# Attention output stage: reversed-half operand for the denominators, tails on GpSimd, and a feature chain moved behind the low parts

## The chip, the cores and the metric

The kernel runs on one core of one Trainium2 chip. A core has a matrix engine (TensorE; PE in the profile, and PEld for its weight loads), three engines for elementwise work (VectorE or DVE, ScalarE or ACT, GpSimd or POOL), queues that start DMA transfers (SP, and also ACT and POOL), the on-chip memory SBUF and the accumulators PSUM. The metric is the time of one execution on the device in microseconds, as the median of several runs.

## The reference

One transformer block with 2048 tokens of width D = 640, in float32. A conditioning vector gives shifts, scales and gates. The attention is linear, with 32 heads of 20 dimensions:

```python
pq = jnp.einsum("bhsd,hdf->bhsf", q, w_phi)
pk = jnp.einsum("bhsd,hdf->bhsf", k, w_phi)
phi_q = jnp.concatenate([_softmax(pq, axis=-1), _softmax(-pq, axis=-1)], axis=-1)
phi_k = jnp.concatenate([_softmax(pk, axis=-1), _softmax(-pk, axis=-1)], axis=-1)
kv = jnp.einsum("bhsf,bhsd->bhfd", phi_k, v)
z  = jnp.einsum("bhsf->bhf", phi_k)
num = jnp.einsum("bhqf,bhfd->bhqd", phi_q, kv)
den = jnp.einsum("bhqf,bhf->bhq", phi_q, z)[..., None] + 1e-6
o = num / den
```

Its output goes through `wo`, a gate and a residual. A second layer norm and a squared-ReLU layer (640 to 1728 to 640) with its own gate and residual follow.

A head's features are two softmaxes, of `pq` and of `-pq`. With unnormalised exponentials `e0`, `e1`, their sums `r0`, `r1`, and the scalar products `d0`, `d1` of the exponentials with `z`, the denominator is `d0/r0 + d1/r1 + 1e-6`. The kernel multiplies it by `r0*r1`, so that one reciprocal is enough: `dd = d0*r1 + d1*r0 + 1e-6*r0*r1`, and the factors for the two halves are `r1/dd` and `r0/dd`. Both the denominators and the factors pair a half with the *other* half's sum: these are the crossed multiplications.

## The kernel before

Tokens are worked in 16 tiles of 128 (`t`), and in 8 pairs of tiles (`j`). Matrix products are made from float32 numbers split into a high and a low part, with three terms each (`three`: high by high, high by low, low by high). Roughly:

- From 0 to 250 us: folding of the weights, normalisation, and K, V, Q projections of all tiles. The exponentials of Q (`e`) of tiles 0 to 11 (`KEPT = 12`) are stored to DRAM (`esp`) and read back as tiles `el`; those of tiles 12 to 15 stay in SBUF (`eq`), and for 13, 14 and 15 the chain of maximum, minimum and subtraction (`q_chain`), the exponentials (`exps`, ScalarE) and the sums (`q_sums`) are made within the next stage.
- From 250 to 385 us: the attention output stage, which the change touches.
- From there to the end: the squared-ReLU layer in 8 pairs (`up`, `acc` in the profile).

The output stage has, for each tile: `e_prod` (L878: the product with `z` into `scr`, its sums per head `dn` on VectorE, then the denominators on GpSimd, L887 to L891), `e_recip` (L897: reciprocal and the two factors, into `dn`, on VectorE), and `e_scale` (L930), which is `e_tail` (L907: heads 30 and 31, 80 columns, into `ut`) and `e_main` (L919: the other 30 heads, 1200 columns, into `ezb`), both on VectorE. For each pair: `tail_turn` and `tail_num` (L936, L943: transpose and product of the tails on TensorE, copies on ScalarE), `tr_e` (L951: transposes of `ezb` on TensorE, copies `ept` on ScalarE), `num` (numerators, into PSUM `numa`, `numb`, `numc`), `num_hi` (ScalarE writes the high parts of `ot`), `num_lo` (the low parts of `ot`: from pair 2 on a subtraction on VectorE, shown as L90, which reads the PSUM tiles last), and `do_wo` (the product of `ot` with `wo` for half `i` of the pair and column group `h`, 15 matmuls each; other TensorE work is hung into it at given terms).

The loop `for j in range(NB)` writes out an order by hand for TensorE, VectorE, ScalarE and GpSimd: each engine does its instructions in the order of the program. SP's queue is ordered by a planner. With `b = 2j+5` and `c = 2j+6`, round `j` issues `e_prod(b)`, `e_recip(b-1)`, `e_scale(b-1)`, `do_wo(j,0,0)` and `(0,1)`, `e_prod(c)`, `e_recip(b)`, `e_scale(b)`, for `j` in 1 and 3 a `q_chain` of tile 13 or 14, then `do_wo(j,1,0)`, `num(j+1)` and `num_hi(j+1)`, and within `do_wo(j,1,1)` `num_lo(j+1)`. The exponentials that follow that `q_chain` come in round `j+1`, behind `do_wo(j+1,0,0)`. In round 5 `q_chain(15)` comes behind the scaling of tile 14. `load_e` reads `el` tiles from DRAM, some three tiles ahead, into buffers that an earlier tile's `e_scale` has to leave first; `plus_x` adds `x` to the stored attention output by a DMA from GpSimd's queue. PSUM's bank `tp` serves `numc` and, next, the tail's transposes.

Of the kernel before, what the change touches and what calls it, by code (L numbers as in the profile page):

```python
# [8 lines left out]
F32 = mybir.dt.float32  # L9
# [3 lines left out]
ALU = mybir.AluOpType  # L13
AX = mybir.AxisListType

P = 128
S = 2048
D = 640
H = 32
DH = 20  # L20
F = 1728
NT = S // P
# [13 lines left out]
KEPT = NT - POSTPONED  # L36
# [1 line left out]
PLAIN = 2  # L38
DEALT = range(NT // 2)
DIRECT = 2  # L40
POWERS = NT
LAST = 3
W_AT = (
    *range(21),
# [9 lines left out]
def kernel(  # L54
# [19 lines left out]
    nc = tc.nc  # L74
# [3 lines left out]
    def mm(o, terms, first=True, last=True, skip=False):  # L78
        for i, (a, b) in enumerate(terms):
            nc.tensor.matmul(  # L80
                o, a, b,
                start=first and i == 0, stop=last and i == len(terms) - 1,
                skip_group_check=skip,
            )

    def three(ah, al, bh, bl):
        return [(ah, bh), (ah, bl), (al, bh)]
# [10 lines left out]
    const = ctx.enter_context(tc.tile_pool(name="const", bufs=1))  # L98
# [79 lines left out]
    rs_q = pc.tile([P, NT, 2 * H], F32, name="rs_q")  # L178
# [80 lines left out]

    cs = const.tile([P, NC], F32, name="cs")  # L260
    ce = const.tile([P, NC], F32, name="ce")
    fill = const.tile([P, 8], F32, name="fill")
    mone = fill[:, :1]
    nc.gpsimd.memset(mone, -1.0)
    nc.scalar.activation(ce, c_t, AF.Exp, scale=-1.0)
    nc.vector.tensor_scalar(ce, ce, 1.0, None, op0=ALU.add)
    nc.vector.reciprocal(ce, ce)
# [169 lines left out]
    def spread(t, e, nm):  # L437
        mx = small([P, 2, H], "mx", f"mx{nm}")
        nc.vector.tensor_reduce(mx[:, 0], heads(t), axis=AX.X, op=ALU.max)
        nc.vector.tensor_reduce(mx[:, 1], heads(t), axis=AX.X, op=ALU.min)  # L440
        for s in (1, 0):
            nc.vector.tensor_tensor(heads(e[:, s]), heads(t), over(mx[:, s]), op=ALU.subtract)
# [32 lines left out]
    def q_chain(t, whole=True):  # L475
        if t < KEPT:
            EQ[t] = tok2(f"q{t % 2}", f"eq{t}")
        e = EQ[t]
        spread(PQ[t], e, f"q{t}")
        if whole:  # L480
            exps(e)
            q_sums(t)
# [232 lines left out]
    for t in range(2, NT - 2):  # L715
        j, i = divmod(t, 2)
# [12 lines left out]
        p = proj("v", t, *([(1, 0, lambda: t1(j + 1, 4))] if t == NT - 3 else []))  # L729
# [136 lines left out]
    def load_e(t):  # L866
        if t >= KEPT:
            if t < NT:
                ET[t] = EQ[t]
            return  # L870
        ET[t] = tok2(("k", "k", f"x{t // 3 % 2}")[t % 3], f"el{t}")
        nc.sync.dma_start(flat(ET[t]), ESP[t])
# [2 lines left out]
    SCR = [flat(tok2("w", f"scr{i}")) for i in range(2)]  # L875
    DN, DD = {}, {}

    def e_prod(t):  # L878
        if t >= NT:
            return  # L880
        z = SCR[t % 2]
        nc.vector.tensor_tensor(z, flat(ET[t]), flat(zb), op=ALU.mult)  # L882
        dn = DN[t] = small([P, 2, H], "dn", f"dn{t}", 3)
        nc.vector.tensor_reduce(dn.rearrange("p s h -> p (s h)"), heads(z), axis=AX.X, op=ALU.add)  # L884
        rs = rs_q[:, t].rearrange("p (s h) -> p s h", s=2)
        dd = DD[t] = small([P, H], "dd", f"dd{t}")
        nc.gpsimd.tensor_tensor(dd, rs[:, 0], rs[:, 1], op=ALU.mult)  # L887
        nc.gpsimd.tensor_scalar(dd, dd, 1e-6, None, op0=ALU.mult)
        for s in range(2):
            nc.gpsimd.tensor_tensor(dn[:, s], dn[:, s], rs[:, 1 - s], op=ALU.mult)  # L890
            nc.gpsimd.tensor_tensor(dd, dd, dn[:, s], op=ALU.add)  # L891
        if t >= POWERS:
            nc.gpsimd.tensor_tensor(dd, dd, mone.to_broadcast([P, H]), op=ALU.pow)
            for s in range(2):
                nc.gpsimd.tensor_tensor(dn[:, s], rs[:, 1 - s], dd, op=ALU.mult)

    def e_recip(t):  # L897
        if t >= NT or t >= POWERS:
            return
        rs = rs_q[:, t].rearrange("p (s h) -> p s h", s=2)  # L900
        nc.vector.reciprocal(DD[t], DD[t])
        for s in range(2):
            nc.vector.tensor_tensor(DN[t][:, s], rs[:, 1 - s], DD[t], op=ALU.mult)

    UT = {}

    def e_tail(t):  # L907
        if t >= NT:
            return
        if t % 2 == 0:  # L910
            u = row("s3", f"ut{t // 2}")
            UT[t], UT[t + 1] = u[:, :80], u[:, 80:160]
        nc.vector.tensor_tensor(
            UT[t].rearrange("p (s h d) -> p s h d", s=2, d=DH),
            ET[t][:, :, 600:].rearrange("p s (h d) -> p s h d", d=DH),
            DN[t][:, :, 30:, None].to_broadcast([P, 2, 2, DH]), op=ALU.mult
        )
# [12 lines left out]
    def e_scale(t):  # L930
        e_tail(t)
        e_main(t)
# [72 lines left out]
    def wo_part(j, i, h, a, b):  # L1005
        t = 2 * j + i
        if h == 0 and a == 0:
            PWO[t] = pj(f"pwo{t}")
            AT[t] = row("s2", f"at{t}")
        s = slice(i * P, (i + 1) * P)  # L1010
        cs_, n = slice(*CUT[h]), CUT[h][1] - CUT[h][0]
        terms = []
        for g in range(5):
            w, o = WO[g], OT[j]
            terms += three(o[:, g, 0, s], o[:, g, 1, s], w[:, 0, cs_], w[:, 1, cs_])
        mm(PWO[t][h][:, :n], terms[a:b], first=(a == 0), last=(b == 15))
        if b == 15:
            nc.scalar.activation(AT[t][:, cs_], PWO[t][h][:, :n], AF.Copy)
            if h:
                nc.scalar.dma_start(A1[t], AT[t])  # L1020
# [199 lines left out]
    SPREAD, SUMS = {1: 1, 3: 2}, {3: 1, 4: 2}  # L1220
    ln0 = None
    for j in range(NB):
        nxt = j + 1 < NB
        b, c = 2 * j + 5, 2 * j + 6
        turns = {1: ((0, 0, 11), (0, 0, 15), (0, 1, 4), (0, 1, 15)), 6: ((0, 1, 2), (0, 1, 8), (0, 1, 15), (1, 0, 15)),
                 0: ((0, 1, 4), (0, 1, 10), (1, 0, 3), (1, 0, 15))}.get(j, ((0, 0, 6), (0, 0, 11), (0, 0, 15), (0, 1, 15)))
        todo_ = (lambda: tail_turn(j + 1), lambda: tail_num(j + 1), lambda: tr_e(j + 1, range(3)), lambda: tr_e(j + 1, (3, 4)))

        def hooks(i, h):
            return [(at, f) for (i_, h_, at), f in zip(turns, todo_) if nxt and (i, h) == (i_, h_)]  # L1230
        if j == 4:
            load_x1(0)
            load_dealt(0)
        if j < 5:
            p_load()
        if j != 5:
            e_prod(b)
        e_recip(b - 1)
        e_scale(b - 1)
        if j == 6:  # L1240
            mod_sum(5, gate_b)
        if j == 5:
            q_chain(KEPT + 3, False)
        load_e(b + 2)
        do_wo(j, 0, 0, *hooks(0, 0))
        if j - 1 in SPREAD:
            exps(EQ[KEPT + SPREAD[j - 1]])
        if j == 5:
            exps(EQ[KEPT + 3])
            q_sums(KEPT + 3)  # L1250
            e_prod(b)
        do_wo(j, 0, 1, *hooks(0, 1))
        if j == 7:
            t2(0, 0)
            t2(0, 1)
        if j == 4:
            ln0 = ln_dealt(0)
            next(ln0)
            next(ln0)
        if j == 6:  # L1260
            next(ln0)
            turn(0, 0)
            turn(0, 1)
        if 1 <= j < 6 and j != 4:
            p_hi()
        if j == 5:
            next(ln0)
        if j in SUMS:
            q_sums(KEPT + SUMS[j])
        e_prod(c)  # L1270
        if j != 5:
            e_recip(b)
            e_scale(b)
        if j in SPREAD:
            q_chain(KEPT + SPREAD[j], False)
        do_wo(j, 1, 0, *hooks(1, 0))
        if j == 7:
            t2(0, 2)
            t2(0, 3)
        if nxt:  # L1280
            num(j + 1)
            num_hi(j + 1)
        if j == 4:
            next(ln0)
            next(ln0)
            next(ln0)
        if j == 5:
            p_hi()
        do_wo(j, 1, 1, b=8)
        if j == 7:  # L1290
            t2(0, 4)
            p = tp("gbt")[:NC, :P]
            nc.tensor.transpose(p, gate_b, ident)
            nc.scalar.activation(gate_r, p, AF.Copy)
            nc.sync.dma_start(GD[1], gate_r)
            nc.sync.dma_start(gb_b, GD[1].rearrange("c p -> (c p)")[None, :].to_broadcast([P, D]))
        if not nxt:
            do_wo(j, 1, 1, a=8)
        if nxt:
            do_wo(j, 1, 1, a=8, b=11)  # L1300
            num_lo(j + 1)
            do_wo(j, 1, 1, a=11)
        if j == 5:
            e_recip(b)
            e_scale(b)
        load_e(c + 2)
        if j:
            plus_x(j - 1)
        if j == 5:
            p_lo(4)  # L1310
            p_load(4)
        if j == 6:
            p_hi(4)
            p_lo(5)
            p_load(3)
        if j == 7:
            p_load(2)
# [485 lines left out]
```

## Time and profile before

| what | value |
|---|---|
| median of 3 runs | 756.0 us (755.9 to 756.18) |
| the profiled execution | 755.36 us, of it the span 753.7 us |
| clock that TensorE was granted | 1.00 |
| DVE, 268 to 302.7 us | 33.42 of 34.70 us busy |
| POOL, 268 to 302.7 us | 21.68 of 34.70 us busy |
| whole span: ACT, POOL | 61%, 23% |

The span is what the hardware profiler recorded on the core; the execution's time has 1.66 us more around it. TensorE is busy for nearly all of the span, and the chain that ended last runs over TensorE for 89% of it and over VectorE for 8%, the latter between 255 and 334 us. In rows of the timeline the first number is the start in us, the second the time from there to the end, then engine, line of the kernel, operation, output and input, shape, the number of instructions merged into the row and, in brackets, how long the engine was idle before it and what ended that.

### The profile page before, as it was taken

What the parts mean: (1) busy time and instruction counts of PE and PEld (TensorE: products, weight loads), DVE (VectorE), ACT (ScalarE), POOL (GpSimd) and SP (SyncE); (2) the same over time, 40 slices, a digit from 0 to 9 for tenths busy, and PEclk for the clock granted to TensorE, in tenths of its full rate; (3) what the DMA queues carried; (4) which work ended last, traced back from release to release, by engine and by line L of the source; (5) the groups of instructions that cost most, each with busy time, mean ns of one, the idle gap of its engine ahead of it and who ended that gap; (6) DMA issues with size and microseconds to landing.
All of it is one profiled execution on the core that took longest, in us unless ns stands there. A gap on an engine that the chain in (4) does not pass through costs nothing.

```text
span 753.7 us, 15321 instructions
## 1 busy us (share of the span) xinstructions
PE 745.8 (99%) x5854; PEld 728.1 (97%) x5854; DVE 604.3 (80%) x1115; ACT 457.3 (61%) x1065; POOL 169.9 (23%) x362
## 2 busy tenths in 40 slices
PE   9999999999999999899999999999999999999998
PEld 9999999999999998789899999999999999999997
DVE  6598987988999899998755768787777776777766
ACT  5767666677863356447677756585574756647431
POOL 3000101000100337646303030132221313213110
PEclk9999999999999999999999999999999999999999
DMA  9811432343432254652986475997677777667460
GB/s 330 331 36 80 154 96 75 106 140 106 140 106 70 71 183 150 154 137 96 208 216 205 132 219 215 281 320 203 187 207 200 212 190 219 187 181 213 129 185 36
DMA packets 58796, 126.39 MB, mean 168 GB/s; under 512 B 7438, under 2 KB 16403, under 8 KB 58723
## 3 DMA queue, kind: packets, MB, share of 16 engines
q1 hardware_dynamic: 38636, 79.20, 32.0%
q0 software_dynamic: 17504, 40.90, 21.9%
q10 hardware_dynamic: 2583, 5.30, 1.9%
q8 instruction: 46, 0.75, 0.4%
q14 instruction: 27, 0.22, 0.1%
HBM read 100.74 MB, written 29.89 MB: 173 GB/s over the span
## 4 chain that ended last, share of the span: by engine, by line
PE 89%; DVE 8%; POOL 1%; ACT 1%; issue 0%; ACTq 0%; POOLq 0%
PE up L80 25%; PE acc L80 18%; PE pk L80 9%; PE pv L80 9%; PE pq L80 8%; PE pwo L80 5%; PE acc3x L80 5%; PE kvp L459 3%; DVE dn L884 2%; DVE scr L882 2%; DVE ezb L924 2%; PE te L958 1%; PE foldk L284 1%; PE ta L366 1%; PE foldq L284 1%; POOL dn L890 1%
## 5 line engine op out<-in xcount | busy, mean ns | idle before, releaser
L80 PE MATMUL up<-h,w 128*128 128x256 f32 x1640 | 204.6, 276 | 0.1
L80 PEld LDWEIGHTS up<-h,w 128*128 128x128 f32 x1640 | 196.4, 188 | 0.7 <-DVE h L90 0.5
L1352 ACT ACTIVATE ft<-up,b_t 128x256 f32<-128x256 f32 x104 | 48.9, 470 | 96.0 <-PE up L80 95.6
L80 PE MATMUL acc<-w,ra 128*128 128x384 f32 x452 | 97.4, 335 | 0.0
L80 PE MATMUL pwo<-wo,ot 128*128 128x384 f32 (+1 forms) x480 | 78.9, 314 | 3.0 <-DVE ot L90 3.0
L1353 DVE TENSOR_TENSOR ft<-ft 128x256 f32<-128x256 f32 x104 | 44.2, 425 | 42.9 <-ACT ft L1352 41.4
L80 PEld LDWEIGHTS pwo<-wo,ot 128*128 128x128 f32 x480 | 69.5, 188 | 6.5 <-DVE ot L90 3.6
L80 PE MATMUL pq<-wq,hT 128*128 128x384 f32 (+1 forms) x480 | 75.6, 312 | 0.0
L80 PEld LDWEIGHTS acc<-w,ra 128*128 128x128 f32 x452 | 72.7, 188 | 0.9 <-DVE ra L90 0.6
L80 PE MATMUL pk<-wk,hT 128*128 128x384 f32 (+1 forms) x480 | 72.7, 308 | 0.0
L80 PEld LDWEIGHTS pq<-wq,hT 128*128 128x128 f32 x480 | 71.1, 188 | 0.6 <-issue 0.2
L80 PE MATMUL pv<-wv,hT 128*128 128x384 f32 (+1 forms) x480 | 71.6, 307 | 0.0
L80 PEld LDWEIGHTS pk<-wk,hT 128*128 128x128 f32 x480 | 70.5, 188 | 0.4 <-issue 0.2
L80 PEld LDWEIGHTS pv<-wv,hT 128*128 128x128 f32 x480 | 70.0, 188 | 0.0
L90 DVE TENSOR_TENSOR ra<-ft,ra 128x384 fp32r<-128x384 f32 (+2 forms) x86 | 36.8, 448 | 32.7 <-ACT ra L1376 20.0
L1462 POOL DMA_DIRECT2D ring_a<-td_a x34 | 18.5, 543 | 117.4 <-PE acc L80 106.3
L1376 ACT ACTIVATE ra<-ft 128x384 fp32r<-128x384 f32 x48 | 25.2, 526 | 28.4 <-DVE ft L1353 22.4
L80 PE MATMUL acc3x<-w,ra 128*128 128x256 f32 x231 | 39.5, 278 | 0.0
L80 PEld LDWEIGHTS acc3x<-w,ra 128*128 128x128 f32 x231 | 37.1, 188 | 0.0
L1367 DVE TENSOR_TENSOR ft<-ft 128x128 f32<-128x128 f32 x136 | 33.3, 286 | 1.2
L450 DVE TENSOR_REDUCE sk<-ek 128x64 f32<-128x1280 f32 x16 | 23.7, 1484 | 12.8 <-ACT ek L445 10.8
L343 POOL TENSOR_SCALAR sma<-sma 128x2 f32<-128x2 f32 x6 | 1.7, 292 | 137.3 <-ACT xb L342 137.3
(270 smaller groups left out, 1475.7 us busy)
## 6 DMA issues: line engine op xcount, KB each, us to landing
ring_c<-td_c POOLq DMA_DIRECT2D x34, 384.0 KB, 3.8
ring_a<-td_a POOLq DMA_DIRECT2D x34, 384.0 KB, 3.5
ring_b<-td_b POOLq DMA_DIRECT2D x34, 256.0 KB, 3.4
esp<-eq SPq DMA_DIRECT2D x12, 640.0 KB
el<-esp SPq DMA_DIRECT2D x12, 640.0 KB
rw<-in_w SPq DMA_DIRECT2D x23, 320.0 KB
wm<-in_w_mod SPq DMA_DIRECT2D x20, 320.0 KB
xb<-in_x SPq DMA_DIRECT2D x8, 640.0 KB
```

Of the source, the lines that this page charges most:

```text
L80: nc.tensor.matmul(o, a, b, start=first and i == 0, stop=last and i == len(terms) - 1, skip_group_check=skip,)
L90: (eng or nc.vector).tensor_tensor(out_lo, full, hi.bitcast(F32), op=ALU.subtract)
L284: nc.tensor.matmul(p[g // 3][:, (g % 3) * 120 : (g % 3) * 120 + n], r, bd_t[:120, g * 120 : g * 120 + n], start=True, stop=True,)
L450: nc.vector.tensor_reduce(s, heads(flat(e)), axis=AX.X, op=ALU.add)
L459: nc.tensor.matmul(kvp[g // 4][64 * c : 64 * c + 64, a : a + 2 * n].rearrange("p (s n) -> p s n", s=2), v[:, u], e[:, :, o : o + n], start ...
L882: nc.vector.tensor_tensor(z, flat(ET[t]), flat(zb), op=ALU.mult)
L884: nc.vector.tensor_reduce(dn.rearrange("p s h -> p (s h)"), heads(z), axis=AX.X, op=ALU.add)
L1352: nc.scalar.activation(r, p, AF.Relu, bias=b1_t[:, f : f + 1])
L1353: nc.vector.tensor_tensor(r, r, r, op=ALU.mult)
L1367: nc.vector.tensor_tensor(t[:, o], t[:, a], t[:, b], op=op)
L1376: nc.scalar.activation(a[:, 0, :3], t[:, :3], AF.Copy)
L1462: nc.gpsimd.dma_start(RING[j, n, r], TD[n][r].bitcast(F32R))
```

## The change

It does six things:

1. In `e_prod` one GpSimd multiplication of 64 elements replaces two of 32: the second operand is read with its halves exchanged (`crossed`).
2. In `e_recip` one VectorE multiplication of 64 elements replaces two of 32, by the same operand.
3. From tile 6 on (`POOL_TAILS`) `e_tail` runs on GpSimd.
4. In `do_wo(j,0,0)` the ten terms with the high part of `ot` come first and the five with its low part last.
5. The `q_chain` of rounds 1 and 3 is issued behind `num_lo` of the round, and that of round 5 ahead of the reciprocal and scaling of tile 14.
6. A path of `e_prod` with powers that no tile took (`POWERS = NT`) goes, with a constant of -1 that GpSimd wrote for it.

```diff
-POWERS = NT
+POOL_TAILS = 6
...
-    fill = const.tile([P, 8], F32, name="fill")
-    mone = fill[:, :1]
-    nc.gpsimd.memset(mone, -1.0)
+    const.tile([P, 8], F32, name="fill")
...
+    def crossed(t):
+        a = rs_q[:, t]
+        return bass.AP(tensor=a.tensor, offset=a.offset + H, ap=[a.ap[0], [-H, 2], [1, H]])
...
+        nc.gpsimd.tensor_tensor(dn, dn, crossed(t), op=ALU.mult)
         for s in range(2):
-            nc.gpsimd.tensor_tensor(dn[:, s], dn[:, s], rs[:, 1 - s], op=ALU.mult)
             nc.gpsimd.tensor_tensor(dd, dd, dn[:, s], op=ALU.add)
...
         nc.vector.reciprocal(DD[t], DD[t])
-        for s in range(2):
-            nc.vector.tensor_tensor(DN[t][:, s], rs[:, 1 - s], DD[t], op=ALU.mult)
+        nc.vector.tensor_tensor(DN[t], crossed(t), DD[t][:, None, :].to_broadcast([P, 2, H]), op=ALU.mult)
...
-        nc.vector.tensor_tensor(
+        (nc.gpsimd if t >= POOL_TAILS else nc.vector).tensor_tensor(
             UT[t].rearrange("p (s h d) -> p s h d", s=2, d=DH),
...
+        if (i, h) == (0, 0):
+            terms = [x for k, x in enumerate(terms) if k % 3 < 2] + terms[2::3]
...
-        if j != 5:
+        if j == 5:
+            q_chain(KEPT + 3, False)
+        else:
             e_prod(b)
         e_recip(b - 1)
         e_scale(b - 1)
...
-        if j == 5:
-            q_chain(KEPT + 3, False)
...
-        if j in SPREAD:
-            q_chain(KEPT + SPREAD[j], False)
         do_wo(j, 1, 0, *hooks(1, 0))
...
         if j == 5:
             e_recip(b)
             e_scale(b)
+        if j in SPREAD:
+            q_chain(KEPT + SPREAD[j], False)
```

More of the change, by code (lines that the diff above doesn't have):

```diff
@@ L888, in e_prod @@
         nc.gpsimd.tensor_scalar(dd, dd, 1e-6, None, op0=ALU.mult)
+        nc.gpsimd.tensor_tensor(dn, dn, crossed(t), op=ALU.mult)
         for s in range(2):
-            nc.gpsimd.tensor_tensor(dn[:, s], dn[:, s], rs[:, 1 - s], op=ALU.mult)
             nc.gpsimd.tensor_tensor(dd, dd, dn[:, s], op=ALU.add)
-        if t >= POWERS:
-            nc.gpsimd.tensor_tensor(dd, dd, mone.to_broadcast([P, H]), op=ALU.pow)
-            for s in range(2):
-                nc.gpsimd.tensor_tensor(dn[:, s], rs[:, 1 - s], dd, op=ALU.mult)
     def e_recip(t):
-        if t >= NT or t >= POWERS:
+        if t >= NT:
             return
-        rs = rs_q[:, t].rearrange("p (s h) -> p s h", s=2)
         nc.vector.reciprocal(DD[t], DD[t])
-        for s in range(2):
-            nc.vector.tensor_tensor(DN[t][:, s], rs[:, 1 - s], DD[t], op=ALU.mult)
+        nc.vector.tensor_tensor(DN[t], crossed(t), DD[t][:, None, :].to_broadcast([P, 2, H]), op=ALU.mult)
     UT = {}
```

## The prediction

> **What bounds the kernel now.** I read the page first: its busy table says that TensorE (PE) works through the whole span.
>
> ```profile
> span 753.7 us, 15321 instructions
> PE 745.8 (99%) x5854; PEld 728.1 (97%) x5854; DVE 604.3 (80%) x1115; ACT 457.3 (61%) x1065; POOL 169.9 (23%) x362
> ```
>
> So an engine that is made faster is worth what TensorE waits for it, and no more. The diff touches only the attention output stage, so I asked next for busy times in stretches of it (engine, busy us, number of instructions; then clock, DMA share and GB/s), and for the waits between 255 and 390 us (who waited for whom: total, times, longest).
>
> ```profile
> 268.00:302.70 34.70, 34.70 (x260) 30.20 (x258) 33.42 (x46) 20.71 (x47) 21.68 (x42) 1.00 0.48 160
> 347.00:364.00 17.00, 17.00 (x129) 15.67 (x128) 14.85 (x24) 12.16 (x28) 13.29 (x31) 1.00 0.49 112
> ```
> ```profile
> PEld pwo L80 <- DVE ot L90: 3.6, 2, 2.8
> PE pwo L80 <- DVE ot L90: 3.0, 2, 2.5
> ```
>
> The columns are PE, PEld, DVE, ACT, POOL. In this stage VectorE (DVE) is nearly as full as TensorE: 33.42 of 34.70 us. TensorE waits for it twice, 3.0 us in total; its weight loads, which run ahead, count 3.6. The timeline shows the two places, and what DVE did just before the first.
>
> ```profile
> 300.39 2.33 PE L80 MATMUL pwo<-wo,ot 128*128 128x256 f32 x17
> 305.18 0.96 PE L80 MATMUL pwo<-wo,ot 128*128 128x384 f32 x4 [2.46 <-DVE ot L90]
> 334.18 0.96 PE L80 MATMUL pwo<-wo,ot 128*128 128x384 f32 x4 [0.53 <-DVE ot L90]
> ```
> ```profile
> 299.34 0.29 DVE L903 TENSOR_TENSOR dn<-rs_q,dd 128x32 f32<-128x32 f32 x2
> 299.67 0.24 DVE L913 TENSOR_TENSOR ut<-el,dn 128x80 f32<-128x80 f32 x1
> 299.83 1.46 DVE L924 TENSOR_TENSOR ezb<-el,dn 128x1200 f32<-128x1200 f32 x1
> 301.21 0.81 DVE L439 TENSOR_REDUCE mxq<-eq 128x32 f32<-128x640 f32 x1
> 304.45 0.68 DVE L90 TENSOR_TENSOR ot<-numa,ot 128x512 fp32r<-128x512 f32 x1
> 305.97 1.48 DVE L882 TENSOR_TENSOR scr<-el,zb 128x1280 f32<-128x1280 f32 x1
> ```
> ```profile
> 299.21 0.60 ACT L981 ACTIVATE ot<-numa 128x512 fp32r<-128x512 f32 x1 [0.53 <-PE numa L80]
> 300.57 0.38 ACT L981 ACTIVATE ot<-numc 128x256 fp32r<-128x256 f32 x1
> 331.50 0.38 ACT L981 ACTIVATE ot<-numc 128x256 fp32r<-128x256 f32 x1
> ```
>
> ScalarE (ACT) had the high parts of `ot` at 299.81 and 300.95. The low parts (L90, `num_lo(2)`) began only at 304.45, because `q_chain(13)` stands ahead of them in DVE's hand-written order: 304.45 - 301.21 = 3.24 us. TensorE has used its last high terms at 300.39 + 2.33 = 302.72 and stands still until 305.18. The second wait is the same thing one `q_chain` later. **The moved `q_chain` is the heart of this change.** The rest frees DVE time.
>
> **The change part by part.**
>
> *Moving `q_chain` behind `num_lo` (j = 1 and 3).* DVE leaves `ezb` of tile 7 at 299.83 + 1.46 = 301.29, earlier still by what the small edits save (below, 0.9): 300.4. `num_lo(2)` takes 305.97 - 304.45 = 1.52, so it ends at 301.9, before TensorE asks at 302.72. The wait of 2.46 goes. Nothing is late in its place at once: `q_chain(13)` runs from 301.9 to 305.2, and the product of tile 9 starts there, not at 305.97. ACT's exponentials of tile 13 come in the next round:
>
> ```profile
> 310.46 0.75 ACT L445 ACTIVATE eq<-eq 128x640 f32<-128x640 f32 x1
> ```
>
> With TensorE 2.46 earlier that is 308.0, 2.8 us after their input is there. If DVE ran later than that, every copy behind them on ACT would wait.
>
> *The order of terms in `do_wo(j, 0, 0)`.* Ten high terms instead of two come before the first low one: no instruction more. It gives `num_lo` eight more matmuls of slack, 8 x 2.62 / 15 = 1.4 us by the chain's row of a run of 15.
>
> ```profile
> 312.45 2.62 PE pwo L80 x15
> ```
>
> By itself it would take 1.4 of the 2.46. Here it is cover for the rounds that follow.
>
> *One operation for two in `e_recip` (16 tiles, DVE).* Two 32-element multiplications and the step to the next cost 299.67 - 299.34 = 0.33. The trace has no 64-element one with a backwards read. Its neighbours are 0.188 (mean) at 32 elements and, above, 0.24 at 80:
>
> ```profile
> L903 DVE TENSOR_TENSOR dn<-rs_q,dd 128x32 f32<-128x32 f32 x32 | 4.7, 188 | 0.5
> ```
>
> Interpolated: 0.22; with the same gap of 0.04 ahead of the next (299.34 + 0.29 to 299.67), 0.26, so 0.07 a tile is saved. From both sides: as cheap as the 32-element one (0.10 saved) or, if the reversed order were read at half speed, as dear as the two together (nothing saved). I take 0.07.
>
> *The tail on GpSimd (POOL) from tile 6 (10 tiles).* DVE's step of 299.83 - 299.67 = 0.16 goes. With the above it is 0.49 - 0.26 = 0.23 a tile. POOL gets a two-input operation of 80 elements; an undisturbed one of 32 takes 0.25, and beside DVE the same kind takes far more:
>
> ```profile
> 293.91 0.25 POOL L890 TENSOR_TENSOR dn<-dn,rs_q 128x32 f32<-128x32 f32 x1 [1.12 <-DVE dn L884]
> 294.49 0.31 POOL L890 TENSOR_TENSOR dn<-dn,rs_q 128x32 f32<-128x32 f32 x1
> 294.88 1.29 POOL L891 TENSOR_TENSOR dd<-dd,dn 128x32 f32<-128x32 f32 x1
> 296.14 1.50 POOL L887 TENSOR_TENSOR dd<-rs_q 128x32 f32<-128x32 f32 x1
> ```
> ```profile
> 294.61 1.46 DVE L924 TENSOR_TENSOR ezb<-el,dn 128x1200 f32<-128x1200 f32 x1
> 295.99 1.54 DVE L882 TENSOR_TENSOR scr<-el,zb 128x1280 f32<-128x1280 f32 x1
> ```
>
> Each POOL operation that meets DVE's `ezb` or `scr` ends just behind it (294.88 + 1.29 = 296.17 beside an `ezb` to 296.07). So a tail costs POOL between 0.3 and 1.5. It stands behind the sums of the next tile in POOL's queue, and so ends up to 3 us after its `ezb` began, when the next `scr` is over. POOL's queue holds: of 299.83 - 294.61 = 5.2 us a tile it has about 1.1 free before its L890. DVE's subtractions out of PSUM don't hold it:
>
> ```profile
> 360.73 0.69 DVE L90 TENSOR_TENSOR ot<-numa,ot 128x512 fp32r<-128x512 f32 x1 [0.47 <-ACT ot L981]
> 360.88 0.25 POOL L890 TENSOR_TENSOR dn<-dn,rs_q 128x32 f32<-128x32 f32 x1
> ```
>  Who waits: the transposes of the tails on TensorE, a round later, and the loads of `el` into the same buffers. For tile 6 the tail is done by 297.6, behind a `scr`; for tile 7, whose `ezb` is followed by `num_lo(2)`, by 300.4 + 0.4 = 300.8. Their transposes come six matmuls after 302.72, at about 303.7. Costed at nothing, with cover of 2.9 us there and 1 us at the tightest place (tile 13, below).
>
> *One POOL operation less in `e_prod`.* 16 x about 0.3 on an engine that is 23% busy: nothing.
>
> *`q_chain(15)` before tile 14's scaling (j = 5).* Both have a round to spare: TensorE shows no wait from 347 to 364. Nothing, at most 1 us if ACT's copies fall behind.
>
> *The removed memset* is 0.1 us of POOL in the first microseconds: nothing.
>
> **The sum.** TensorE wins 2.46 + 0.53 = 2.99 if DVE keeps up. I followed DVE through the rounds:
>
> ```profile
> 318.56 1.48 DVE L882 TENSOR_TENSOR scr<-el,zb 128x1280 f32<-128x1280 f32 x1
> 330.28 0.81 DVE L439 TENSOR_REDUCE mxq<-eq 128x32 f32<-128x640 f32 x1
> 334.98 1.48 DVE L882 TENSOR_TENSOR scr<-eq,zb 128x1280 f32<-128x1280 f32 x1
> 340.87 1.49 DVE L487 TENSOR_REDUCE rs_q<-eq 128x64 f32<-128x1280 f32 x1 [0.66 <-ACT eq L446]
> 348.64 0.41 DVE L90 TENSOR_TENSOR ot<-numc,ot 128x256 fp32r<-128x256 f32 x1
> ```
> ```profile
> 349.17 0.38 PE L940 MATMUL tail<-ident,ut 128*80 128x128 f32 x2
> ```
>
> Up to 301.29 it saves 6 x 0.07 + 2 x 0.23 = 0.9, and each later round 2 x 0.23 = 0.46. Round 2: 305.2 + (318.56 - 305.97) - 0.46 = 317.3 at most (waits for ACT in it shrink too, perhaps to 316.8). Round 3: another 11.72 - 0.46 brings 328.1 to 328.6. There `num_lo(4)` must wait for ACT, whose last high part comes at 331.88 - 2.46 = 329.4; DVE is through at about 330.1, and with the `q_chain` (334.98 - 330.28 less 1.52 = 3.2) starts the next round at 333.3, not 334.98. Round 4 takes 349.05 - 334.98 = 14.07, less 0.46, less the 0.66 for ACT: `num_lo(5)` ends at 346.25. TensorE, 2.99 earlier, comes to the transpose of tail pair 6 at 349.17 - 2.99 = 346.18, and it needs the PSUM bank that `num_lo(5)` reads last. The two meet: a wait of 0.1 to 0.2 there. I take 2.9 us off. Behind 347 TensorE had no wait, ACT and DVE are not full, and the weights' loads follow DVE's releases; all of it moves forward together.
>
> The profiled execution took 755.36 us (span 753.7 and 1.66 around it), 0.64 below the median 756.0. By its own time: 755.36 - 2.9 = 752.5; against the median **753.1 us**, 0.38% less. A difference under 0.2%, 1.5 us, is about what a measurement of this kernel can't tell from none.
>
> **The rivals.**
>
> *The gain is eaten by the port (same).* What is seen in the rows is POOL waiting for DVE. The other way round, DVE's `scr` took 1.54 beside POOL work and 1.48 without, 0.06 more. If each POOL tail slipped in ahead of a big DVE operation and held it for its own 0.34, DVE would lose 0.34 for tiles 6 to 13 by round 4: 2.7 us. `num_lo(5)` would end at 349.0, TensorE would wait 2.7 at the tail's transpose, and the time would be 755.8; with half of it, 754.4. For it: DVE and TensorE meet there in any case. Against it: the 0.06. [...]
>
> *A load comes late (slower).* The tails of tiles 6 and 7 now also hold the buffers into which `el` of tiles 9 and 10 is loaded. Now these are issued as `ezb` ends:
>
> ```profile
> 296.09 5.54 SPq L872 DMA_DIRECT2D el<-esp  x2
> 308.50:309.50 1.00, 1.00 (x12) 1.00 (x11) 0.97 (x4) 0.92 (x2) 0.36 (x2) 1.00 0.62 126
> 311.14 1.54 DVE L882 TENSOR_TENSOR scr<-el,zb 128x1280 f32<-128x1280 f32 x1
> ```
>
> The second is issued at 296.09 + 5.54 - 0.33, or 301.3; the DMA traffic that it shares with others thins out in the stretch from 308.5 to 309.5 (share 0.62), and tile 10's product reads it at 311.14 (at 310.1 in the changed kernel). I have the tail of tile 7 done at 300.8, so the load keeps its time. Were it held until `scr` of tile 9 had passed, it would be issued at 306.7 and land up to 8.2 later, near 315; DVE would be 4.8 late, TensorE would wait about 4.7 by tail pair 6, and the sum be 3.0 gained and 4.7 lost: 757.7. It decides from an issue about 1 us later than now, and turns the sign from about 4.
>
> *Something behind the stage does not move along (between).* The weights for the next phase are on their way while this one ends, and ACT waits for them once:
>
> ```profile
> 377.42 1.37 ACT L1050 ACTIVATE w<-rawt 128x640 fp32r<-128x640 f32 x2 [0.40 <-DMA rw<-in_w]
> ```
>
> If they landed when they do now, ACT would be held almost 3 us and the start of the next phase with it, all but what its copies can catch up: 755.4 if that is 0.6. Against it: DVE frees their buffers some 3 us earlier too. A part of it, 1 to 2 us, is likelier than all.
>
> **How the numbers follow.** The forecast, 752.4 to 754.2, has 0.69; its low end is 756.0 less the 3.6 of the weight loads' wait. The port has 0.15 (754.4 to 755.8), the transfers 0.10 (754.2 to 755.4), the late load 0.06 (756.5 to 758). Below 754.5: 0.69, half of the port's and half of the transfers', 0.81; above 757.5: some 0.04; the rest 0.15. The range from 752.4 to 755.5 leaves out less than 0.2.
>
> **What would show it.** Right: no wait of `pwo` for DVE `ot` near 302 and 331; `num_lo(2)` directly behind `ezb` of tile 7; `dn` of 64 elements near 0.22; POOL tails of 0.3 to 1.5. Wrong: waits at a `tail` transpose or at a `scr` for DMA, DVE operations stretched by 0.3 beside POOL, or a later ACT `w` wait.

## The result and the profile after

The changed kernel takes 751.55 us (median of 6 runs, 751.01 to 752.85) beside 756.09 us before (6 runs, 755.4 to 756.7); the ratio is 0.9941 with a 95% interval of 0.9928 to 0.9954. That is 4.5 us less, where 2.9 was forecast and 752.4 was the low end of the range. The profiled executions differ by less: 751.83 against 755.36 us.

The page of the changed kernel (span; busy time and number of instructions by engine):

```profile
span 750.1 us, 15320 instructions
PE 744.9 (99%) x5854; PEld 728.3 (97%) x5854; DVE 601.4 (80%) x1089; ACT 457.5 (61%) x1065; POOL 169.0 (23%) x355
```

Of the list of waits between 255 and 390 us, what TensorE and its weight loads still wait for:

```profile
PEld tail L936 <- POOL rn L1160: 0.7, 1, 0.7
PE tail L936 <- POOL rn L1160: 0.4, 1, 0.4
```

Both waits of `pwo` for `ot` are gone. The wait left is at the transpose of tail pair 6. The timeline of DVE at the place of the old 2.46 us wait:

```profile
298.72 1.41 DVE L920 TENSOR_TENSOR ezb<-el,dn 128x1200 f32<-128x1200 f32 x1
300.05 0.68 DVE L90 TENSOR_TENSOR ot<-numa,ot 128x512 fp32r<-128x512 f32 x1
301.25 0.41 DVE L90 TENSOR_TENSOR ot<-numc,ot 128x256 fp32r<-128x256 f32 x1
301.58 0.81 DVE L437 TENSOR_REDUCE mxq<-eq 128x32 f32<-128x640 f32 x1
```

The low parts now come straight behind `ezb` of tile 7, and the chain of tile 13 (L437) behind them. TensorE's timeline at both old waits, after and then before:

```profile
300.12 3.09 PE L80 MATMUL pwo<-wo,ot 128*128 128x256 f32 x21
303.05 0.38 PE L936 MATMUL tail<-ident,ut 128*80 128x128 f32 x2
...
328.31 3.09 PE L80 MATMUL pwo<-wo,ot 128*128 128x256 f32 x21
331.24 0.38 PE L936 MATMUL tail<-ident,ut 128*80 128x128 f32 x2
```
```profile
306.11 0.42 PE L940 MATMUL tail<-ident,ut 128*80 128x128 f32 x2
306.28 1.12 PE L80 MATMUL pwo<-wo,ot 128*128 128x384 f32 x5
...
331.32 2.33 PE L80 MATMUL pwo<-wo,ot 128*128 128x256 f32 x17
...
335.11 0.41 PE L940 MATMUL tail<-ident,ut 128*80 128x128 f32 x2
```

The same 21 matmuls lie between the first row and the transpose. Before, that took 306.11 - 300.39 = 5.72 us, and now 303.05 - 300.12 = 2.93: 2.79 are won where the recorded idle time was 2.46. In round 4 it is 3.79 against 2.93: 0.86 for 0.53. **Each wait cost 0.33 us more than its idle time.** A part of that is a second wait for DVE, which the list of waits before has in a row of its own. Below it, from the timelines before, the weight load of the transpose and DVE's last low part:

```profile
PEld tail L940 <- DVE ot L90: 0.6, 2, 0.3
```
```profile
306.11 0.15 PEld L940 LDWEIGHTS tail<-ident,ut 128*80 128x80 f32 x2 [0.29 <-DVE ot L90]
```
```profile
305.64 0.41 DVE L90 TENSOR_TENSOR ot<-numc,ot 128x256 fp32r<-128x256 f32 x1
```

The transpose needs the bank that the last low part reads, and starts 0.47 us after the start of that operation (306.11 - 305.64), in round 4 as well (335.11 - 334.64). By the single starts in the trace it comes 0.31 us behind the start of the last of the four matmuls, where the changed kernel has 0.17: that is some 0.13 of the 0.33. Most of the rest lies at the first matmul behind the wait, whose successor starts 0.28 and not 0.18 behind it, and in the way idle time is counted, from the end of a matmul beside which the next would have begun: the two ahead of the wait start 0.17 us apart and take 0.33 and 0.34 each.

### The profile page after: what moved, and what is told of

It is laid out like the page before. It is cut to its first block, busy times and chain, and to the rows that moved or that the text cites. A ratio compares the mean times of both kernels' runs of the same rounds, so it can differ in the third digit from the quotient of the medians.

```text
span 750.1 us, 15320 instructions
## 1 busy us (share of the span) xinstructions
PE 744.9 (99%) x5854; PEld 728.3 (97%) x5854; DVE 601.4 (80%) x1089; ACT 457.5 (61%) x1065; POOL 169.0 (23%) x355
## 4 chain that ended last, share of the span: by engine, by line
PE 98%; ACT 1%; DVE 1%; POOL 0%; issue 0%; ACTq 0%; POOLq 0%
PE up L80 25%; PE acc L80 18%; PE pq L80 9%; PE pk L80 9%; PE pv L80 9%; PE pwo L80 9%; PE acc3x L80 5%; PE kvp L457 3%; PE te L954 2%; PE numa L80 1%; PE foldk L282 1%; PE numb L80 1%; PE ta L364 1%; PE foldq L282 1%; PE warm L625 1%; PE mrow L586 1%
```

## The experiments

Theory A, formed from these rows: the waits were priced too low, at 3.0 and not at 2.79 + 0.86 = 3.65, and the rest is spread between runs. Theory B: the saved operations are worth about 1.5 us that no wait shows.

### The changed kernel again

No edit.

> The changed kernel once more, beside the kernel before on the same chip. Theory A (the waits were priced too low: each of the two cost TensorE its recorded idle time and about 0.3 us more, until weight loads and matmuls overlap again, so 3.6 us and not 3.0 are won, and 0.6 is lost at the transpose of tail pair 6; the rest of the 4.5 us is spread between runs): 3.5 to 4.0 us under the kernel before, and the two profiles differ by the same. Theory B (another part of the change is worth about 1.5 us that the profile's waits don't show): 4.3 us or more under it, here too.

Measured: 751.69 us beside 755.95, 4.3 less (ratio 0.9938, 0.9926 to 0.9951). That is more than the 3.5 to 4.0 of theory A, and what theory B expected (4.3 or more). Something was missing in A.

### The chains moved back

```diff
+        if j in SPREAD:
+            q_chain(KEPT + SPREAD[j], False)
         do_wo(j, 1, 0, *hooks(1, 0))
...
             e_scale(b)
-        if j in SPREAD:
-            q_chain(KEPT + SPREAD[j], False)
```

> The changed kernel with the feature chains of tiles 13 and 14 back ahead of the low parts; all else stays. Theory A: in round 2 TensorE waits about 2 us again, and not at the first low term, which the new order of terms has moved back, but at the transpose of tail pair 3, which stands six terms into the product and needs the PSUM bank that the low parts release; later DVE is no longer the last to come. 1.7 to 2.6 us slower than the changed kernel, 1.2 to 2.0 under the kernel before. Theory B (the operations saved on DVE make the gain): under 1 us slower than the changed kernel. The prediction's own sum would give 3.0 less the slack of eight terms and 0.9 of DVE's time: about 0.7 us slower.

Measured: 755.2 us, 3.5 slower than the changed kernel, where theory A had 1.7 to 2.6; against before 0.9986 (0.9977 to 0.9994). Theory B is out: with every saved operation in place, the gain is nearly gone. The place of the wait is as expected, its price is not. TensorE's timeline:

```profile
304.50 0.39 PE L936 MATMUL tail<-ident,ut 128*80 128x128 f32 x2 [1.89 <-DVE ot L90]
304.65 1.76 PE L80 MATMUL pwo<-wo,ot 128*128 128x384 f32 x5
306.21 0.91 PE L942 MATMUL tail<-kvd,ept 80*128 80x40 f32 x4
306.91 1.57 PE L80 MATMUL pwo<-wo,ot 128*128 128x384 f32 x4
```

The wait stands at the transpose, six terms into the product. But the matmuls behind it are slow: 1.76 us for five that took 1.12 before. Busy times by stretch say why (the number behind POOL's is the granted clock):

```profile
304.50:305.00 0.50, 0.49 (x4) 0.50 (x5) 0.50 (x1) 0.07 (x1) 0.00 (x0) 0.89 0.97 147
305.00:306.00 1.00, 1.00 (x5) 1.00 (x4) 0.90 (x2) 0.31 (x1) 0.00 (x0) 0.50 0.88 137
307.00:308.00 1.00, 1.00 (x4) 1.00 (x4) 0.93 (x4) 0.30 (x2) 0.49 (x2) 0.50 0.97 255
308.00:309.00 1.00, 1.00 (x9) 0.92 (x9) 1.00 (x1) 0.47 (x2) 0.92 (x2) 0.85 0.19 42
```

**TensorE's clock falls to 0.50** from about 304.9 to 308.3, 3.4 us; it begins 0.4 us after work has begun again. The profile of the kernel before shows 1.00 throughout its span. So theory A became A': idle time, plus 0.33 us, plus a fall of the clock in some executions.

### The move alone, and with the order of terms

The first takes the kernel before and moves the two chains; the second takes the changed kernel, with two operations in `e_recip` and `POOL_TAILS = NT`, so that DVE saves nothing.

> The kernel before with only the two feature chains moved behind the low parts; no operation is saved and no tail is on GpSimd. Theory A: the wait of 2.46 in round 2 goes with its 0.3, but DVE has lost the time for it: it comes about 2 us late to the low parts of pair 5, and TensorE waits for these at the transpose of tail pair 6. 1.0 to 2.0 us under the kernel before. If the move alone were the gain: 3.0 us or more under it. Theory B: under 1 us.

Measured: 753.5 us, 2.45 under before (ratio 0.9965, 0.9953 to 0.9977).

> The changed kernel with the factors by two operations again and all tails on DVE: the moved chains and the order of terms stay, DVE saves nothing. Theory A: as with the move alone, within 0.4 us, because the order of terms gives no slack where a transpose six terms in waits for the bank: 1.0 to 2.0 us under the kernel before. If the order of terms were worth its eight matmuls: 2.4 to 3.0 us under it. Theory B: 1 us or less.

Measured: 752.92 us, 3.0 under before (0.996, 0.9947 to 0.9972). Both gain more than expected. A' accounts for it: from the first transposes of `ezb` (`te`) to the first `up`, the first profile before takes 117.8 us and these two take 116.0 and 115.7, so 1.8 and 2.1 less; with the 0.7 for the clock that is worked out below it makes 2.5 and 2.8. Their order among themselves isn't clear. Their lists of waits, the move alone first, show that DVE is late again further on:

```profile
PE pwo L80 <- DVE ot L90: 1.3, 2, 1.1
```
```profile
PE tail L938 <- DVE ot L90: 1.7, 2, 1.2
```

The move removes the long wait. Without the saved operations a part of it comes back in rounds 3 and 5, as 1.3 and 1.7 us. The saved operations pay by keeping DVE ahead of that.

### The kernel before once more

> The kernel before once more, for its profile. Theory A': besides idle time and overlap, the wait of about 2.5 us in round 2 lets TensorE's clock fall to 0.50 for some 3.4 us in part of the executions (the profile with the chains moved back showed 0.50 from about 304.9 to 308.2 and matmuls 1.6 us longer there; the profile of before did not). Then a profile of the kernel before that shows 0.50 behind the wait has a span about 1.6 us longer than one that doesn't, and the median lies between the two. Theory B': the clock never falls in the kernel before, and the spread of 755.0 to 757.5 is the start of the kernel (transfers) alone.

Measured: 756.65 us beside 756.28 (ratio 1.0007, 0.9997 to 1.0017). Its profile, by stretch and in TensorE's timeline:

```profile
306.00:307.00 1.00, 1.00 (x5) 1.00 (x4) 0.96 (x2) 0.38 (x1) 0.00 (x0) 0.50 0.98 267
307.00:308.00 1.00, 1.00 (x6) 1.00 (x5) 1.00 (x1) 0.00 (x0) 0.00 (x0) 0.50 1.10 256
```
```profile
304.46 0.97 PE L80 MATMUL pwo<-wo,ot 128*128 128x384 f32 x4 [2.42 <-DVE ot L90]
305.39 0.65 PE L940 MATMUL tail<-ident,ut 128*80 128x128 f32 x2
305.69 1.95 PE L80 MATMUL pwo<-wo,ot 128*128 128x384 f32 x5
```

Same program, same wait, and this time the clock falls behind it: the five matmuls take 1.95 us and not 1.12. From TensorE's first `pk` to the end this execution is 1.23 us longer than the first profile. Its span is only 0.5 longer, since the start of the kernel, with its loads, was 0.73 us shorter in it.

The clock's records in the traces show where the two executions differ. In the three profiles with a fall behind a wait (this one, the chains moved back, and the made wait below) it lasts 3413 ns, and it begins 300.373, 300.373 and 372.053 us after the clock was first full: 88, 88 and 109 times 3413.3 ns. In the first profile before and in that of the changed kernel the clock stays full for 747.519 and 744.106 us, up to a fall behind the last matmul: 219 and 218 times. So each of these five falls began a whole number of stretches of that length (windows, from here on) after the first full clock, and the stretches lay differently against the program in the two executions of the kernel before. What sets the clock no run shows. The window that holds the pause and the next one, in this profile:

```profile
301.97:305.38 3.41, 0.99 (x5) 0.65 (x4) 3.34 (x7) 0.14 (x1) 1.89 (x3) 1.00 0.93 232
305.39:308.79 3.40, 3.40 (x14) 3.38 (x14) 3.33 (x5) 0.68 (x3) 0.38 (x2) 0.50 1.00 222
```

In the first profile a boundary falls into the pause, at 303.87; that follows from its own fall behind the end of the program, at 754.42, which is 132 windows later:

```profile
300.45:303.86 3.41, 2.27 (x19) 1.96 (x17) 3.34 (x5) 0.88 (x3) 3.32 (x5) 1.00 0.42 126
303.87:307.28 3.41, 2.10 (x12) 1.81 (x13) 3.41 (x5) 0.38 (x1) 0.81 (x1) 1.00 1.02 223
754.43:755.40 0.97, 0.00 (x0) 0.00 (x0) 0.00 (x0) 0.00 (x0) 0.00 (x0) 0.50 0.00 0
```

Here TensorE works 0.99 us of the window, and the next one gets half the clock. There the boundary cuts the pause in two, TensorE works 2.27 and 2.10 us, and the clock stays up. In the three profiles with a fall behind a wait the window ahead of it holds 1.89 us of idle time (the chains moved back), 2.42 (this one) and 2.2 (the made wait). In the first profile before the most that a window holds while TensorE still has work is 1.32, in that of the changed kernel 0.9, and no 0.50 follows. The other nine profiles, whose longest recorded waits are 1.2 us, have a mean clock of 0.999 or more.

Each timed execution has its mean clock beside it. 0.5 for 3.4 of 754 us makes 0.998, and so the executions fall into two groups:

| kernel | longest recorded TensorE wait in the stage, us | executions | clock 0.998 or less | median of those | median at 0.999 or more |
|---|---|---|---|---|---|
| before (beside the experiments, three chips) | 2.46 | 55 | 33 | 756.6 | 755.42 |
| chains moved back | 1.89 | 11 | 7 | 755.22 | 754.04 |
| made wait (below) | 2.67 | 10 | 9 | 756.98 | 754.82 (one) |
| move and terms | 1.2 | 6 | 0 | | 752.92 |
| move alone | 1.1 | 5 | 0 | | 753.5 |
| before, wait filled (below) | 0.5 | 11 | 0 | | 754.84 |
| changed (the result and two runs) | 0.5 | 16 | 0 | | 751.7 |

The run above, of the kernel before once more, is not in the table; of its eight executions seven have 0.998 or less. In the kernel before three executions of five have the lower clock, and their median is 1.2 us longer. The first profile had caught one that doesn't.

### The wait filled

The kernel before, with matmuls whose results are not needed, ahead of the third term of round 2:

```diff
+    def keep_warm(j):
+        for _ in range(22):
+            nc.tensor.matmul(PWO[2 * j][1][:, :P], neg, neg, start=True, stop=True)
...
-        do_wo(j, 0, 0, *hooks(0, 0))
+        do_wo(j, 0, 0, *([(2, lambda: keep_warm(j))] if j == 2 else []), *hooks(0, 0))
```

> The kernel before with 22 matmuls of 128 columns that compute nothing needed, put into the wait of 2.46 us in round 2 (into a PSUM bank that is written anew afterwards). More work, and the low parts come no sooner. Theory A': TensorE doesn't rest, so no execution loses clock and the weight loads stay overlapped: 0.3 us under the kernel before if its clock seldom falls, 1.0 to 1.5 under it if it falls in half of the executions or more; no 0.50 in the profile. Theory B' (only the arrival of the low parts counts): equal to the kernel before within 0.3 us, or slower by what the filling overshoots.

Measured: 754.84 us beside 756.28, 1.4 less (ratio 0.9983, 0.9974 to 0.9992), no execution with a reduced clock.

```profile
302.76 2.57 PE L1224 MATMUL pwo<-neg 128*128 128x128 f32 x22
305.61 0.97 PE L80 MATMUL pwo<-wo,ot 128*128 128x384 f32 x4 [0.28 <-DVE ot L90]
```

The low parts come no sooner, and 22 matmuls more make the kernel faster. What they buy is the clock: its share of the gap, 0.6 x 1.2 = 0.7 us. Some 0.6 to 0.7 more stay open. They are not the 0.33, for the four matmuls behind the filling still take 0.97, and the stage is no shorter than in the first profile before, which has the full clock too (118.0 and 117.8 us from the first `te` to the first `up`). The single executions lie between 754.3 and 756.5.

### A made wait

The changed kernel, with six reductions of no use on DVE ahead of the low parts of pair 7:

```diff
+            if j == 6:
+                for k in range(6):
+                    nc.vector.tensor_reduce(small([P, 64], "dly", f"dly{k}", 1), rs_q.rearrange("p t (a b) -> p (t a) b", b=16), axis=AX.X, op=ALU.add)
             num_lo(j + 1)
```

> The changed kernel with six additional DVE reductions of 1024 elements (about 7.5 us in all, results unused) ahead of the low parts of pair 7, where DVE has about 5 us to spare: a made wait of TensorE at the first low term of round 7, about 3 us long. Theory A': the time grows by the recorded idle time and about 0.3 us, and by about 1.6 us more in executions whose clock falls: 4.5 to 5.0 us over the changed kernel if it falls in most. Theory B': it grows by the idle time alone, about 3 us.

Measured: 756.86 us, and the clock reduced in nine of ten executions. Beside it ran the kernel before (756.28), not the changed one; over the 751.7 of the changed kernel in the table it is 5.2.

```profile
377.74 8.27 PE L80 MATMUL pwo<-wo,ot 128*128 128x384 f32 x43 [2.67 <-DVE ot L90]
```
```profile
380.00:382.50 2.50, 2.50 (x14) 2.50 (x13) 2.29 (x4) 0.08 (x1) 0.22 (x1) 0.53 0.65 74
```

A recorded wait of 2.67 us cost about twice its length here, in another round and behind another cause than in the kernel before. That is 0.2 us above the range of theory A'. From the first `te` to the first `up` the profile has 119.4 us, the changed kernel 114.5: 4.9 more.

### The parts that are left

All of these ran beside the changed kernel on one chip, and the later transpose before that on another one, without the changed kernel. The one GpSimd multiplication less, the earlier `q_chain(15)` and the removed memset were not run alone.

> The changed kernel beside the next three on one chip. Theory A' (idle time, 0.33 us of lost overlap behind each wait, and a clock that falls behind a wait of 1.9 us and more in about two of three executions): the clock is full in all its executions; in the kernel before it is reduced in about two of three, those are some 1.1 us longer, and the changed kernel lies 3.6 to 4.0 us under the others. If the clock had nothing to do with it: the two groups of the kernel before don't differ.

Measured: 752.18 us beside 756.3 (0.9945, 0.9932 to 0.9957); clock full in all five.

```diff
-                 0: ((0, 1, 4), (0, 1, 10), (1, 0, 3), (1, 0, 15))}.get(
+                 0: ((0, 1, 4), (0, 1, 10), (1, 0, 3), (1, 0, 15)), 5: ((0, 0, 11), (0, 0, 15), (0, 1, 4), (0, 1, 15))}.get(
```

> The changed kernel with the transposes of tail pair 6 at the eleventh term of round 5's first product and not at the sixth, as round 1 has it (the later hooks of the round move with it). If TensorE's wait of 0.37 there (0.57 with its overlap) is for the PSUM bank that DVE's last low part releases, or for GpSimd, five matmuls (0.9 us) cover it: 0.3 to 0.6 us under the changed kernel, no wait at the transpose. If the wait comes back at the next hook, no change.

> The changed kernel with the transposes of tail pair 6 five terms later, against the changed kernel on the same chip. Its profile before showed no wait there and a stage about 0.45 us shorter; if that is so, the median is 0.3 to 0.6 us under the changed kernel's; if the spread between executions hides it, within 0.3.

Measured: 751.97 us on the other chip (before there: 756.28), and 752.12 against the changed kernel's 752.18 on the common one. The wait at the transpose is gone, and a smaller one stands at the second group of transposes:

```profile
351.17 1.14 PE L954 MATMUL te<-ident,ezb 128*124 128x128 f32 x8 [0.17 <-ACT ept L955]
```

Whether it gains the 0.3 to 0.6 us can't be told from the spread; it isn't a version that is shown to be better.

> The changed kernel with the old order of terms. Theory A': only in round 5 do the low parts come so late that the third term has to wait, 0.3 us, and then the transpose of the tails has that much less to wait; in round 0 the low part comes 0.1 late. 0.1 to 0.5 us slower than the changed kernel, clock full. If the order gives the eight matmuls of cover that the prediction gave it: 0.5 to 1.4 us slower.

Measured: 751.69 us with the old order of terms, 0.5 under the changed kernel and within its spread (751.6 to 754.4 beside 751.25 to 753.17). Neither the expected 0.1 to 0.5 us nor the prediction's slack can be seen. Its list of waits has one row for DVE's `ot`, `PEld` alone:

```profile
PEld pwo L80 <- DVE ot L90: 0.4, 1, 0.4
```

> The changed kernel with all tails on DVE, and nothing else undone. DVE does 0.16 to 0.2 us more per tile from tile 6 on, and GpSimd no longer works beside its large operations. Theory A': low parts of pair 5 come 1.0 to 1.3 us later, and TensorE waits that much longer at the transpose of tail pair 6, in all 0.8 to 1.4 us slower than the changed kernel, clock full. If GpSimd's tails cost DVE the port, as the prediction's rival has it: no slower, or faster.

Measured: 752.91 us with all tails on DVE, 0.7 slower where 0.8 to 1.4 were expected; the spreads overlap, but its profile shows the mechanism:

```profile
346.17 0.41 PE L936 MATMUL tail<-ident,ut 128*80 128x128 f32 x2 [1.08 <-DVE ot L90]
```

The wait at tail pair 6 grows from 0.37 to 1.08 and ends with DVE's low part; the tails on DVE are the only edit, and they make TensorE wait 0.7 us longer there. GpSimd as a burden to DVE would have shown the contrary.

## Why the prediction was wrong

**The step that failed** is the first line of its sum: "TensorE wins 2.46 + 0.53 = 2.99 if DVE keeps up." The mechanism was right and the waits went. Their price was mis-sized, by two things.

- Each of the two waits cost 0.33 us beyond its idle time. From the timelines: 2.79 and 0.86, together 3.65, in part (0.13 us of each 0.33) because the transpose waits for the last low part once more. The row for the weight loads, 3.6 us, came close in advance; the prediction had it in a fence and used it as the low end of the range instead of as the term. The row for the transpose, 0.6 us, it left out.
- The wait of 2.46 us also came with a lower clock in 33 of 55 executions, whose median is 1.2 us longer: 0.7 us in the mean. The one profile of before, in which a window boundary cuts the pause in two, showed a clock of 1.00, so no view of it had this in it. It is why the profiled execution, at 755.36, lay 0.64 below the median (at full clock that is 755.42): the prediction noted that distance and took it for an offset that would stay.

The account then closes but for 0.3 us. At full clock: 3.65, less 0.57 at tail pair 6 (0.37 of idle time and 0.2 beyond it), and 0.1 to 0.2 each before round 2 and behind round 6 make 3.4. The profiles agree: from the first `te` to the first `up`, 117.8 us before, and 114.5, 114.4 and 114.4 in three of the changed kernel. The medians at full clock are 755.42 and 751.7, 3.7 apart. With 0.7 for the clock that is 4.4, beside 4.5, 4.3 and 4.1 in the three comparisons. The last 0.3 is inside the spread: between profiles of the same code the start of the kernel differs by up to 0.7 us, and the part from the first `up` to the end by up to 1.3.

Point by point:

- **What bounds the kernel**: right. The changes of time that the profiles show within the stage are changes of TensorE's waits, or of its clock behind them.
- **The moved chains**: right in place. `num_lo(2)` was put at 300.4 to 301.9 and ran from 300.05 to 301.66. Moved back alone, 3.5 us are lost.
- **The order of terms**: wrong. "It gives `num_lo` eight more matmuls of slack" overlooks that the transposes of the tails stand at the sixth term and need the bank that the last low part frees; the kernel before had its second wait there, the chain moved back waited there, and the old order costs nothing that can be measured.
- **One operation for two in `e_recip`**: right, 0.22 to 0.23 for 64 elements read in reverse halves.

```profile
293.38 0.23 DVE L899 TENSOR_TENSOR dn<-rs_q,dd 128x64 f32<-128x64 f32 x1
295.04 1.54 DVE L884 TENSOR_TENSOR scr<-el,zb 128x1280 f32<-128x1280 f32 x1
```

- **The tails on GpSimd**: right. The two kinds are there, behind a `scr` and ahead of the low parts; beside them `scr` takes the same 1.54 as before (row above). The rival by the port, which no run shows, didn't happen, nor did the one by the late load: no `scr` waited for a transfer.

```profile
295.19 1.57 POOL L909 TENSOR_TENSOR ut<-el,dn 128x80 f32<-128x80 f32 x1
...
300.20 0.32 POOL L909 TENSOR_TENSOR ut<-el,dn 128x80 f32<-128x80 f32 x1
```

- **The meeting at tail pair 6**: right in place and a little small, 0.37 (0.57 by the later start of the transpose) and not 0.1 to 0.2. The list names GpSimd's `rn`, an operation that has nothing to do with the tails. It is DVE: the transpose began 0.55 to 0.56 us after the start of the last low part in three profiles of the changed code, whatever `rn` did. One of them, the kernel with the made wait, has DVE in the bracket. TensorE's row and DVE's, in the changed kernel:

```profile
345.87 0.39 PE L936 MATMUL tail<-ident,ut 128*80 128x128 f32 x2 [0.37 <-POOL rn L1160]
```
```profile
345.31 0.41 DVE L90 TENSOR_TENSOR ot<-numc,ot 128x256 fp32r<-128x256 f32 x1
```

- **Behind the stage everything moved along**: right. From the first `up` to the end it is the same within 0.1 us in the two profiles.

## What to carry to other kernels

A wait of the engine that bounds the kernel can cost more than its idle time, here 2.79 us for 2.46: look whether what stands behind it waits for the same engine again, in the rows of the weight loads too. For waits like the 1.9 to 2.7 us here ask whether the clock behind them stayed up in every execution, not in the profiled one alone. Where a median lies off the profiled execution, look at the clocks of the single executions before taking the distance for an offset. When slack is counted up to the operand that is late, look also at what else in between needs the same buffer: here a transpose at the sixth term made ten early terms useless.

## What was not expected of the hardware

Behind pauses of TensorE of 1.89, 2.42 and 2.67 us three profiles show its clock at 0.50 for 3.4 us, and in the kernels with these pauses 7 of 11, 33 of 55 and 9 of 10 executions have a mean clock of 0.998 or less; with pauses of up to 1.2 us none of the 38 in the table has. By the windows of 3413 ns, 1.89, 2.42 and 2.2 us of idle time lay in the one ahead of the fall; a pause of 2.46 us that a boundary cut into 1.14 and 1.32 left the clock at 1.00. The fall began with the next window, in the three profiles 0.4, 0.9 and 1.2 us after work had begun again. Matmuls without use, put into the pause, kept the clock full in 11 of 11 executions and made the kernel 1.4 us faster.
